# Order of issue and buffers of a linear-attention and Mish block taken from tables in place of a planner and pools

## The chip, the core and the metric

The kernel runs on one core of a Trainium2 chip. The metric is the device time of one execution in microseconds (us); lower is better. Before the change, three runs took 489.09, 489.33 and 489.36 us (median 489.33).

Engines are named as in the profile: PE is the matrix engine (PEld its weight loads), DVE the vector engine, ACT the scalar engine, POOL the general engine, SP the engine whose queue issues the DMAs. Each engine takes its instructions strictly in the order in which they were issued, and waits at the head of its queue until semaphores of the others let the next one go.

## What is computed

S is 2048 tokens, D 512, H 32 heads of 16, F 1792. In float32:

```python
xn = layernorm(x)
q, k, v = split(xn @ wqkv)                      # 32 heads of 16
phi(u) = [softmax(u @ w_phi), softmax(-u @ w_phi)]
kv = phi(k).T @ v ;  z = sum over tokens of phi(k)
o = (phi(q) @ kv) / (phi(q) @ z + 1e-6)
s = o @ wo
g = silu(mish(xn @ w1 + b1) @ w2)
out = x + s * g
```

## The kernel before

Tokens are worked on in 16 tiles of 128 (NT), and for the large products in pairs of tiles or in groups of 512. Each large product is taken in 2x2 blocks with seven block products in place of eight, and each float32 operand is split into a high and a low part of type fp32r (on ACT a copy to `...h`, on DVE or POOL the rest to `...l`), so that one block product is six matmuls: two halves of the contraction by three (low x high, high x low, high x high). Plain float32 matmuls are used for folding `w_phi` into the weights (`wkf`, `wqf`: a weight block times the block-diagonal `phit`), for transposes (`pt`), for `kvp` and for `pn`.

The program is written as parts, each a function of a tile or block number. In the order of the data:

- `N` normalizes a tile of x and transposes it (`pt`); the seven block operands of a pair of tiles are `fh`/`fl` (first and second group of 512 tokens) or `xc`.
- `kh`, `kl`, `wv`, `kd`, `ks`, `k2`, `k4` prepare the seven weight blocks for k and v, `wq` and `wQ` those for q. `wq` folds two chunks (`wqf`, through PSUM and an ACT copy) and stores them.
- `Ka` to `Kd` are the k and v products of a pair (banks `kx`, `ky`, `kz`; `kj` for the pair that is taken directly), with the softmax; `A` sums phi(k) and, for every second pair, multiplies into `kvp`. `z` ends the sums.
- `Q` is the q product of a pair of tiles (banks `qx`, `qy`, `qz`), its seven block products numbered Q.0, .2, .4, .6, .8, .10 and .12; `D` the denominator; `Ua`/`Ub` the numerator (`pn`, out into `oh` and `ol`); `O` the projection by wo (`pw`, stored as `so`).
- `P` prepares and `M` reloads the w1 blocks, `Fa` to `Fd` are the first product of the MLP (banks `fx`, `fy`, `fz`), stored raw as `hd`; `R` prepares w2.
- `G` is a step of the second product: `r` is loaded from `hd`, ACT applies Mish, three subtractions and sums make seven operands (`r` to `r`), then `ah` on ACT and `al` on DVE or POOL, and seven groups of matmuls into the `y` banks. `E` adds the banks up (`yc`, `yy`) and applies silu, `H` multiplies by `s`, adds x and stores. For the last 256 tokens one call, `G49`, does the seven sums in one pass at the end, and `E7` ends the four pieces one by one (`u`, `xx`).

What is recorded first is not yet an order. Every call on an engine goes to `Program.call`, which makes an operation of it; `one()` puts several calls into one operation, or gives one operation two possible engines (`either`: DVE or POOL; `copy`: ACT or DVE). Then `Program.order` decides. It hands PE its operations in the order of ORDER, the written list of parts; the other engines are filled by `simulate`, a list scheduler that plays the program with a cost for each operation (`cost`), due times (`late`, moved by the numbers in SHIFT), limits on free buffers (`fits`), a guard time for the port that DVE and POOL share, and a model of the DMA queue. What it returns, sorted by its start times, is issued. Where it has put an operation on POOL less than 4000 ns after the last DVE operation that takes two SBUF inputs (or the like) ends, `issue` adds a wait for that DVE operation.

Buffers come from pools: 8 PSUM banks under one tag, 38 large slots (`slot`), 15 of 2 KB (`s2`), and some small ones. The framework decides which buffer of its tag a tile gets.

Of the kernel before, what the change touches and what calls it, by code (L numbers as in the profile page):

```python
# [28 lines left out]
PEN, HOLD, MARGIN, GUARD = 0, 300, 1000, 140  # L29
BACK, COLD, DRATE, LANES, SWITCH = 2650, 3400, 400, 8, 230  # L30
READ, WRITE, STALL, AHEAD_PE = 1150, 150, 1500, 110
BLOCK, HEAD, FETCH, IDLE = 256, 89, 5200, 2100
BEGIN = {"PE": 1100, "V": 900, "G": 2300, "A": 800, "Q": 800}

SLOTS, S2 = 38,15
SLACK, AHEAD, LAT = 15000, 40000, 150
WAKE, EACH, NEAR = 15, 2, 4000
# [11 lines left out]
SHIFT = """  # L49
kd:0:-9100 wv1:0:-1100 N1:2:-15000 N1:3:300 N1:5:5800 N1:13:4300 N1:14:-7000 kl:3:-10000 Ka2:3:-9700 N5:6:-2200  # L50
N5:8:-1200 N5:11:13000 N2:0:-3500 N2:2:-2000 N3:4:1500 N3:13:-11400 Kc0:7:4900 Kc0:10:14200 k4:0:-6900 Kd0:6:300
N6:14:-6700 P0:1:4800 P0:5:3800 P0:11:5000 Kb1:3:300 N7:6:-2800 N7:8:7300 N7:9:-6400 N8:8:-2700 N9:13:3600 Kc1:8:1800
Kd1:4:-7300 N10:3:-300 N11:0:5800 P4:0:-7000 P4:4:300 P4:5:3100 N14:8:-6800 Kd3:1:-5000 Kd3:6:-6400 A2:0:-3600
N13:5:-2500 Fa4:1:-1100 Fa4:3:3600 N15:4:10800 N15:6:-5000 N15:11:-300 Kc5:6:4400 Ka6:1:-600 Kc6:5:-300 Kc6:6:2600
P6:6:-1100 P6:8:5100 P3:3:-2600 P3:11:-2000 Kb7:1:2800 Fa3:1:-300 Fa3:3:300 P2:4:-2000 P2:6:1100 P2:10:800 Kd6:6:-8800
Kd6:9:-9500 Fb6:3:-2300 Fc3:1:1600 Fc3:2:800 Fc3:4:7900 wQ:1:2300 wQ:13:6600 Fa2:3:300 Fa2:4:-1900 Fa1:3:900
M4:1:-1400 P5:10:3200 Q0:7:14700 Q0:23:-2000 z:4:1200 z:5:11100 D0:0:800 D0:4:4700 D0:8:-800 L:5:-4200 L:9:-3000
D1:2:-8100 Q1:16:800 Q1:19:300 Q2:3:-15000 Q2:9:-2500 Q2:15:300 Q2:25:-1900 Q3:17:-4300 Q3:18:4700 Fc5:5:9400
D3:7:1800 D4:3:-4000 D4:4:6800 D4:5:1300 D4:6:11900 D4:10:11500 D5:1:-300 Fb11:1:-4700 Q4:7:-600 Q4:16:600 Q4:18:7800
Q4:20:800 Q4:21:-1400 Q4:23:-8800 Q5:25:-600 M3:1:-5000 M3:2:-6700 Fa12:1:800 D6:6:-500 D6:10:300 Fb10:1:-500  # L60
D7:1:5000 D7:4:6600 D8:1:-2400 D8:4:-500 D8:10:1400 Q6:1:4700 D9:10:800 Q7:1:7800 Q7:16:-4700 Q7:20:4800 Q7:21:-13000
Q7:23:-12900 M2:2:-5000 D10:6:-800 M6:2:-4100 D11:1:-1700 Ua0:1:-1100 Ua0:12:-800 Fc9:1:3400 D12:5:-5000 D13:0:-4400
D13:4:12500 Fa13:4:800 Ub0:14:-4300 wo0:1:-4500 Fc13:4:-13100 Fc7:2:15000 R0:8:4700 D14:6:-7800 O3:2:-900 Ua1:2:-4200
Ua1:4:-6700 Ua1:6:-3100 Ua1:11:-5000 Ua1:13:-300 Ua1:14:300 O5:2:-500 Fd13:2:-4200 O6:1:-2200 Ub1:5:-5000 Ub1:6:-2000
Ub1:8:-4500 G7:4:-2000 R2:0:-2200 R1:1:15000 R1:6:4200 R1:10:5800 G8:3:-5000 G8:6:1900 O11:2:-2000 R6:1:4900 R3:2:1600
R3:8:-3300 R4:1:2000 G11:0:-6800 G12:5:3100 G12:6:-1200 G13:5:-1100 G32:3:6500 G34:6:4000 G1:4:-15000 G3:0:5000
G4:0:-4100 G5:5:4000 G35:3:9300 G35:4:-5800 G35:6:3100 G14:0:-10200 G14:3:4000 E0:6:-2600 G15:2:800 G39:6:-300
G16:4:-5000 G41:3:1700 E5:4:-300 G20:0:800 G20:2:-2000 G20:3:-5300 G20:6:-5000 G42:3:5100 G42:5:-300 G43:2:4200
G44:2:300 G44:4:-2000 H4:2:1300 G46:3:6600 G46:6:300 G24:6:500 G47:5:-3000 G26:4:-1600 E6:2:-800 G49:0:-5000
G49:2:4000 G49:6:-1100 G49:9:2000 G49:12:-2200 G49:19:2200 G49:26:5000 G49:31:800 G49:36:2800 G49:42:-4700 G49:43:800  # L70
E7:9:-300 E7:10:15000 H3:7:2300 H6:8:800
"""
ACT_SET = {AF.Exp: 1, AF.Silu: 3, AF.Mish: 2}


class Op:
    __slots__ = ("impl", "reads", "writes", "at", "idx", "succ", "ndep", "late", "new", "ready", "start", "eng", "sets", "slack", "open", "soon", "pos", "deps", "lock", "part", "half", "code", "tiles", "shift")


class Program:  # L80


    def __init__(self, nc):
        self.eng = {"PE": nc.tensor, "V": nc.vector, "G": nc.gpsimd, "A": nc.scalar, "Q": nc.sync}
        self.ops, self.tag, self.cap, self.pe = [], {}, {}, []
        self.group, self.slack, self.part, self.half = None, SLACK, None, False
        self.region, self.count = {}, {}
        self.shifts = {k: int(v) for k, _, v in (c.rpartition(":") for c in SHIFT.split())}

    @staticmethod  # L90
    def cost(e, m, a, k):
        aps = [v for v in a if isinstance(v, bass.AP)]
        n = aps[0].free_size()
        if e == "PE":
            if m == "transpose":
                return 109
            n, c = aps[2].free_size(), aps[1].free_size()
            if aps[1].dtype == F32R:
                return max(n / 2.4 + 0.104 * c, c * 0.835 + 2)
            full = 2 * max(n / 1.2 + 2.5, c * 0.835)  # L100
            if aps[1].shape[0] == 32:
                return max(0.155 * n, 24)
            return max(full * aps[0].shape[0] / P, 27)
        if e == "Q":
            return 450
# [29 lines left out]
    def add(self, impl, reads, writes, sets=()):  # L135
# [10 lines left out]
        if "PE" in impl:  # L146
            self.pe.append(o)
# [1092 lines left out]
```

## Time and profile before

| | before |
|---|---|
| median of 3 runs | 489.33 us |
| span of the profiled execution (first to last instruction) | 488.7 us |
| PE busy | 480.2 us (98%) |
| DVE busy | 446.2 us (91%) |
| ACT busy | 293.4 us (60%) |
| POOL busy | 267.2 us (55%) |
| DMA, mean over the span | 216 GB/s, 105.70 MB |

The page gives no time for the profiled execution other than its span.

In the rows below, the timeline has start (us), duration (us), engine, line, operation, what is written from what, shape, and in brackets the idle time before and what ended it. The chain of waits has start, duration, engine and tile. A row of a stretch has the stretch, its length, the busy time of PE, PEld, DVE, ACT and POOL in this order, the granted PE clock (1.00 is full), the share of time that the DMA engines were busy, and GB/s. A row of a group has the count, then the busy time and the mean of one in ns, or shortest, median and longest in ns. Nearly all work is recorded by one helper, so it carries that helper's line (L404), and one goes by the names of the tiles.

### The profile page before, as it was taken

To read this page: it belongs to the slowest core of one execution; us is meant where nothing else is said; L and a number is where in the kernel's file an instruction comes from. 1 tells how busy PE (TensorE), PEld (TensorE's weight loads), DVE (VectorE), ACT (ScalarE), POOL (GpSimd) and SP (SyncE) were. 2 spreads that over 40 slices of the span, in tenths; PEclk is the share of its full clock that TensorE was granted. 3 is DMA by queue.
4 is the path that set the end of the run, shared out by engine and by line. 5 is a ranking of instruction groups with operands and counts; after the bars stand their busy time and mean duration, and the time that the engine had idled before them with its cause. 6 is when DMAs were issued, how large, how long until landed. Compare 5 with 4: busy or idle time off the path is not lost.

```text
span 488.7 us, 10325 instructions
## 1 busy us (share of the span) xinstructions
PE 480.2 (98%) x3820; PEld 426.2 (87%) x3820; DVE 446.2 (91%) x893; ACT 293.4 (60%) x453; POOL 267.2 (55%) x197
## 2 busy tenths in 40 slices
PE   8899999999999999999999999999999999999996
PEld 7788888888887889898887878788899999999996
DVE  6999999988899999999999899889989889999894
ACT  3997545654556453635345545677879687777631
POOL 3989998998490446798987686370021024120030
PEclk9999999999999999999999999999999999999999
DMA  8812923968867689982959635726465646578172
GB/s 294 265 48 109 332 99 122 312 197 272 315 217 313 225 301 345 394 300 87 310 199 341 229 115 211 261 85 207 141 193 165 201 154 211 194 234 269 44 250 94
DMA packets 68641, 105.70 MB, mean 216 GB/s; under 512 B 6896, under 2 KB 37744, under 8 KB 68592
## 3 DMA queue, kind: packets, MB, share of 16 engines
q1 hardware_dynamic: 68448, 104.79, 62.9%
q8 instruction: 30, 0.49, 0.4%
q10 hardware_dynamic: 144, 0.26, 0.2%
q14 instruction: 19, 0.16, 0.1%
HBM read 60.60 MB, written 44.43 MB: 215 GB/s over the span
## 4 chain that ended last, share of the span: by engine, by line
PE 81%; DVE 8%; DMA 5%; issue 2%; ACT 1%; SPq 1%; POOL 1%; DVEq 0%; ACTq 0%
PE y L404 20%; PE fx L404 14%; PE pw L404 9%; PE kx L404 7%; PE fy L404 7%; PE qx L404 5%; PE ky L404 3%; PE fz L404 3%; PE qy L404 2%; PE kj L404 2%; PE pn L404 2%; PE kz L404 2%; DVE al L404 2%; DMA wvr<-wv 1%; DMA w1a<-w 1%
## 5 line engine op out<-in xcount | busy, mean ns | idle before, releaser
L404 POOL TENSOR_TENSOR al<-r,ah 128x896 fp32r<-128x896 f32 x8 | 17.0, 2130 | 87.4 <-DMA r<-hd 35.1
L404 ACT ACTIVATE ah<-r 128x896 fp32r<-128x896 f32 x56 | 50.9, 944 | 16.0 <-DVE r L404 12.9
L404 DVE TENSOR_TENSOR al<-r,ah 128x896 fp32r<-128x896 f32 x48 | 54.8, 1171 | 5.0 <-ACT ah L404 3.2
L404 DVE TENSOR_TENSOR r<-r 128x128 f32<-128x128 f32 (+1 forms) x157 | 48.3, 353 | 5.0 <-ACT r L404 3.4
L404 PE MATMUL y<-w2h,al 128*128 128x256 f32 x160 | 45.4, 283 | 0.0
L404 PE MATMUL y<-w2h,ah 128*128 128x256 f32 x160 | 45.3, 283 | 0.0
L404 PE MATMUL y<-w2l,ah 128*128 128x256 f32 x160 | 45.3, 283 | 0.0
L404 PE MATMUL y<-w2t,ah 128*128 128x256 f32 x224 | 41.0, 283 | 0.0
L404 PE MATMUL fx<-fh,w1b 128*128 128x512 f32 x112 | 38.8, 393 | 0.0
L404 ACT ACTIVATE r<-r 128x512 f32<-128x512 f32 x56 | 33.2, 621 | 7.9 <-DMA r<-hd 7.9
L404 PEld LDWEIGHTS y<-w2t,ah 128*128 128x128 f32 x224 | 34.9, 192 | 0.0
L404 PE MATMUL y<-w2t,al 128*128 128x256 f32 x112 | 31.7, 283 | 0.0
L404 PEld LDWEIGHTS y<-w2h,al 128*128 128x128 f32 x160 | 30.7, 192 | 0.6 <-issue 0.4
L404 PEld LDWEIGHTS y<-w2l,ah 128*128 128x128 f32 x160 | 30.7, 192 | 0.2
L404 PEld LDWEIGHTS y<-w2h,ah 128*128 128x128 f32 x160 | 30.7, 192 | 0.0
L404 PE MATMUL y<-w2g,ah 128*128 128x256 f32 x160 | 30.4, 283 | 0.0
L404 PEld LDWEIGHTS fx<-fh,w1b 128*128 128x128 f32 x112 | 21.0, 188 | 5.4 <-issue 1.2
L404 PEld LDWEIGHTS y<-w2g,ah 128*128 128x128 f32 x160 | 25.0, 192 | 0.0
L404 POOL TENSOR_TENSOR r<-r 128x128 f32<-128x128 f32 (+1 forms) x11 | 6.4, 592 | 32.3 <-DMA sr<-so 22.5
L404 PE MATMUL y<-w2g,al 128*128 128x256 f32 x80 | 22.6, 283 | 0.0
L404 ACT ACT_TABLE_LOAD x13 | 16.7, 1283 | 9.2 <-DMA x<-x 4.1
L404 PE MATMUL fx<-fl,w1b 128*128 128x512 f32 x56 | 21.8, 390 | 0.0
(766 smaller groups left out, 1730.0 us busy)
## 6 DMA issues: line engine op xcount, KB each, us to landing
r<-hd SPq DMA_DIRECT2D x56, 256.0 KB, 3.5
xd<-xc SPq DMA_DIRECT2D x8, 896.0 KB, 4.1
w1b<-w1d SPq DMA_DIRECT2D x14, 512.0 KB, 5.5
w1b<-w1d SPq DMA_DIRECT2D x14, 384.0 KB, 4.9
so<-so SPq DMA_DIRECT2D x16, 256.0 KB, 2.1
x<-x SPq DMA_DIRECT2D x15, 256.0 KB, 3.7
w1a<-w SPq DMA_DIRECT2D x7, 512.0 KB, 4.6
w1d<-w1sh SPq DMA_DIRECT2D x7, 512.0 KB, 2.9
```

Of the source, the lines that this page charges most:

```text
L404: ins = getattr(e, m)(*a, **k)
```

## The change

The scheduler goes. A table PLAN names every one of the 2454 operations in the order in which it is issued, over all engines, with a letter for the engine where there is a choice; a table PLACE names the buffer of every tile, tag by tag, in the order in which the tiles are made. Pools have one buffer per tag, and there is a tag for each buffer. The operations, their shapes and their number are the same; ORDER still sets in which order they are recorded (and so the buffer numbers in names), no longer that of PE.

```diff
-SLACK, AHEAD, LAT = 15000, 40000, 150
-WAKE, EACH, NEAR = 15, 2, 4000
+WAKE, EACH, NEAR = 15, 2, 24
...
-SHIFT = """
-kd:0:-9100 wv1:0:-1100 N1:2:-15000 N1:3:300 N1:5:5800 N1:13:4300 N1:14:-7000 kl:3:-10000 Ka2:3:-9700 N5:6:-2200
...
+PLAN = """
+N1.0 @.0 @.1 N4.0 @.2 @.3 @.15 @.4 N4.3 @.5 @.17 @.6 N0.0 @.7 N1.1 @.8 wv0.0 @.9 @.10 N1.2 @.11 @.16G N4.1 N1.3 @.12
...
+PLACE = {
+    "ps": """
+7 1 6 3 4 2 5 1 7 0 6 1 3 7 3 7 7 3 5 1 7 2 1 5 0 2 4 0 7 3 7 1 4 2 5 0 6 7 5 3 0 3 7 4 5 3 2 4 7 3 5 4 2 5 3 6 7 2 0
...
     def order(self):
-        at = [0]
-        for o in self.pe:
-            at.append(at[-1] + o.impl["PE"][0])
-        self.links()
-        return self.simulate(at)
...
+        at = {o.name: o for o in self.ops}
+        plan = []
+        for c in PLAN.split():
+            e = c[-1] if c[-1] in self.eng else ""
+            o = at.pop(c[:-1] if e else c)
+            o.eng = e or next(iter(o.impl))
+            plan.append(o)
...
     def issue(self, tc):
         first, held = True, None
-        for o in self.order():
-            for i, (m, a, k) in enumerate(o.impl[o.eng][1]):
+        for n, o in enumerate(self.order()):
+            for i, (m, a, k) in enumerate(o.impl[o.eng]):
...
-                if i == 0 and o.eng == "G" and held is not None and o.start - held[1] < NEAR:
+                if i == 0 and o.eng == "G" and m != "dma_start" and held is not None and n - held[1] < NEAR:
...
-    psum = ctx.enter_context(tc.tile_pool(name="psum", bufs=8, space=bass.MemoryType.PSUM))
+    psum = ctx.enter_context(tc.tile_pool(name="psum", bufs=1, space=bass.MemoryType.PSUM))
+    place = {t: iter(c.split()) for t, c in PLACE.items()}
...
-        pools[tag] = ctx.enter_context(tc.tile_pool(name=tag, bufs=n))
-        prog.cap[tag] = n
+        pools[tag] = ctx.enter_context(tc.tile_pool(name=tag, bufs=n if tag == "st" else 1))
...
-        t = psum.tile(shape, F32, tag="ps", name=name)
+        t = psum.tile(shape, F32, tag="ps" + next(place["ps"]), name=name)
...
-        t = pools[tag].tile(shape, dtype, tag=tag, name=name)
+        t = pools[tag].tile(shape, dtype, tag=tag if tag == "st" else tag + next(place[tag]), name=name)
```

The removed functions `cost`, `records`, `halves`, `links`, `simulate`, `volume`, `reads` and `bcast` served the scheduler alone. The wait of POOL for DVE is now added where at most 23 places of the list lie between the two.

131 operations change engine: 67 go from DVE to POOL, 42 from POOL to DVE, 13 from ACT to DVE, 9 from DVE to ACT. In the second product of the MLP, 47 sums and subtractions of `r` stand on POOL where 11 stood (36 of them 128x128, 11 of 128x256, against 6 and 5), and 1 split `al` where 8 stood. On PE about half of the operations keep their order among themselves; the others move, mostly by a few places, and by about 30 at most.

**Three places in the order.** The first is the start. The next two pieces are the first loads in SP's queue, before and now (x0 to x5 are tiles of x, wkT00 to wkT11 the four loads of wk, wvr0 and wvr1 the two halves of wv).

```order
L404 DMA x4_151<-x 128x512
L404 DMA x5_153<-x 128x512
L404 DMA phic_100<-phi 128x64
L404 DMA x0_164<-x 128x512
L404 DMA wkT00_137<-wqkT 128x512
L404 DMA wkT01_138<-wqkT 128x512
L404 DMA wvr0_141<-wv 128x2x512
L404 DMA wkT10_139<-wqkT 128x512
L404 DMA wvr1_159<-wv 128x2x512
L404 DMA wkT11_140<-wqkT 128x512
L404 DMA x2_202<-x 128x512
L404 DMA wqT10_190<-wqkT 128x2x512
```

```order
L294 DMA x4_151<-x 128x512
L294 DMA phic_100<-phi 128x64
L294 DMA x5_153<-x 128x512
L294 DMA wkT00_137<-wqkT 128x512
L294 DMA x0_164<-x 128x512
L294 DMA wvr0_141<-wv 128x2x512
L294 DMA wkT01_138<-wqkT 128x512
L294 DMA wkT10_139<-wqkT 128x512
L294 DMA wvr1_159<-wv 128x2x512
L294 DMA wkT11_140<-wqkT 128x512
L294 DMA wqT10_190<-wqkT 128x2x512
```

The first half of wv has moved ahead of wkT01, phic and wkT00 each by one place, and wqT10 ahead of x2.

On PE, in the same stretch, these are the first rows, before and now (wake keeps PE busy while nothing else is there).

```order
L404 MATMUL wake_99<-ones_84 128x128 x15
L404 MATMUL wkf01_147<-phit_101,wkT00_137 128x128 x4
L404 MATMUL wkf11_148<-phit_101,wkT01_138 128x128 x4
L404 MATMUL pt4_156<-ident_83,x4_151 128x128 x4
L404 MATMUL pt0_167<-ident_83,x0_164 128x128 x4
L404 MATMUL pt1_173<-ident_83,x1_170 128x128 x4
L404 MATMUL wkf21_181<-phit_101,wkT10_139 128x128 x4
L404 MATMUL wkf31_182<-phit_101,wkT11_140 128x128 x4
L404 MATMUL pt5_184<-ident_83,x5_153 128x128 x4
L404 MATMUL kx2_187<-wv0h_142,fl00_104 128x512
```

```order
L294 MATMUL wake_99<-ones_84 128x128 x13
L294 MATMUL wkf01_147<-phit_101,wkT00_137 128x128 x4
L294 MATMUL wake_99<-ones_84 128x128 x2
L294 MATMUL pt1_173<-ident_83,x1_170 128x128 x4
L294 MATMUL pt4_156<-ident_83,x4_151 128x128 x4
L294 MATMUL wkf11_148<-phit_101,wkT01_138 128x128 x4
L294 MATMUL pt0_167<-ident_83,x0_164 128x128 x4
L294 MATMUL wkf21_181<-phit_101,wkT10_139 128x128 x4
L294 MATMUL pt5_184<-ident_83,x5_153 128x128 x4
L294 MATMUL wkf31_182<-phit_101,wkT11_140 128x128 x4
L294 MATMUL kx2_187<-wv0h_142,fl00_104 128x512
```

The transpose pt5 has moved ahead of the last fold of wk (wkf31). A few rows on, still on PE, the two folds of wq stood one behind the other between kz2 and kj00; the piece before and the piece now:

```order
L404 MATMUL kz2_188<-wv1h_160,fl10_106 128x512
L404 MATMUL kz2_188<-wv1l_161,fh10_105 128x512
L404 MATMUL kz2_188<-wv1h_160,fh10_105 128x512
L404 MATMUL wqf21_192<-phit_101,wqT10_190 128x128 x4
L404 MATMUL wqf31_193<-phit_101,wqT10_190 128x128 x4
L404 MATMUL kj00_194<-wv0h_142,fl00_104 128x512
```

```order
L294 MATMUL kx2_187<-wv0h_142,fh00_103 128x512
L294 MATMUL wqf21_192<-phit_101,wqT10_190 128x128 x4
L294 MATMUL kz2_188<-wv1h_160,fl10_106 128x512
L294 MATMUL kz2_188<-wv1l_161,fh10_105 128x512
L294 MATMUL kz2_188<-wv1h_160,fh10_105 128x512
```

The fold wqf21 has moved ahead of kz2, and wqf31 is gone from here: it stands 18 matmuls after kz2, in the middle of kj03.

The second place is the q product on PE. Here is the end of the block of the first pair before (its last two block products, qy0 and qx0, one behind the other):

```order
L404 MATMUL qy0_525<-wqs1h_493,fl20_108 128x256
L404 MATMUL qy0_525<-wqs1l_494,fh20_107 128x256
L404 MATMUL qy0_525<-wqs1h_493,fh20_107 128x256
L404 MATMUL qx0_523<-wq1h_489,fl60_116 128x256
L404 MATMUL qx0_523<-wq1l_490,fh60_115 128x256
```

and what follows the same qy0 now:

```order
L294 MATMUL qy0_525<-wqs1h_493,fh20_107 128x256
L294 MATMUL fx2_512<-fh50_113,w1sl2_502 128x512
L294 MATMUL fx2_512<-fl50_114,w1sh2_501 128x512
L294 MATMUL fx2_512<-fh50_113,w1sh2_501 128x512
L294 MATMUL fx2_512<-fh50_113,w1sl2_502 128x512
L294 MATMUL fx2_512<-fl50_114,w1sh2_501 128x512
L294 MATMUL fx2_512<-fh50_113,w1sh2_501 128x512
L294 MATMUL qy2_606<-wqs0h_491,fl30_110 128x256
```

A block product of the MLP and one of another pair stand between, then qz0 and another of the MLP, before the last product of qx0 comes. The eight q blocks are mixed with the MLP in this way throughout.

The third place is on DVE, where the last numerator block (pn11) is split into the operands of the projection (ol), before and now.

```order
L404 TENSOR_TENSOR ol31_903<-pn11_1_897,oh31_902 128x8x32
L404 TENSOR_TENSOR ol21_901<-pn11_3_899,oh21_900 128x8x32
L404 TENSOR_TENSOR ol31_903<-pn11_2_898,oh31_902 128x8x32
L404 TENSOR_TENSOR w2m4_893<-w2e4_895,w2m4_893 128x256
L404 TENSOR_TENSOR ol31_903<-pn11_3_899,oh31_902 128x8x32
L404 TENSOR_TENSOR al1_2_937<-r1_2_935,ah1_2_936 128x896
```

```order
L294 TENSOR_TENSOR ol31_903<-pn11_1_897,oh31_902 128x8x32
L294 TENSOR_TENSOR ol21_901<-pn11_3_899,oh21_900 128x8x32
L294 TENSOR_TENSOR ol30_886<-pn10_3_882,oh30_885 128x8x32
L294 TENSOR_TENSOR r1_3_940<-r1_3_940 128x2x128
L294 TENSOR_TENSOR w2r6_927<-w2r6_927 128x256
L294 TENSOR_TENSOR ol31_903<-pn11_2_898,oh31_902 128x8x32
L294 TENSOR_TENSOR r4_1_970<-r4_1_970 128x2x128
L294 TENSOR_TENSOR w2e3_916<-w2r3_915,w2e3_916 128x256
L294 TENSOR_TENSOR r1_2_935<-r1_2_935 128x128
L294 TENSOR_TENSOR w2e6_928<-w2r6_927,w2e6_928 128x256
L294 TENSOR_TENSOR ol31_903<-pn11_3_899,oh31_902 128x8x32
```

The last piece of ol31 stood two places behind the one of pn11_2; now four other rows stand between, and it is the 605th row of DVE where it was the 587th. On PE the projections of tiles 8, 9, 12 and 15, which read ol21 and ol31, stand directly behind the first two steps of the second product, where only that of tile 8 and then 14 and 13 stood.

In the last stretch, E7's two copies of the first y bank go from ACT to DVE, and on DVE the sum for the third of the four last pieces (`u15_1`) is the ninth row from the end, where it was the fifth.

More of the change, by code (lines that the diff above doesn't have):

```diff
@@ L1 @@
 from contextlib import ExitStack, contextmanager
-import heapq
 import numpy as np
@@ L55 @@
[L55 to L64, printed above, removed]
@@ L76 @@
+E7.30
+"""
+PLACE = {
+    "ps": """
[4 rows of a table added]
+""",
+    "s2": """
[4 rows of a table added]
+""",
+    "slot": """
[11 rows of a table added]
+""",
+    "sm": """
[3 rows of a table added]
+""",
+    "tq": """
+1 0 1 0 0 1 0 1 0 1
+""",
+    "rq": """
+7 6 2 5 3 4 1 0 7 6 5 4 2 3 0 1
+""",
+}
 class Op:
-    __slots__ = ("impl", "reads", "writes", "at", "idx", "succ", "ndep", "late", "new", "ready", "start", "eng", "sets", "slack", "open", "soon", "pos", "deps", "lock", "part", "half", "code", "tiles", "shift")
+    __slots__ = ("impl", "reads", "writes", "idx", "name", "eng", "lock")
@@ L408, in issue @@
             if o.eng == "V" and "V" in o.lock:
-                held = ins.ins.name, o.start + o.impl["V"][0]
+                held = ins.ins.name, n
 def locks(e, m, a):
```

432 lines of the change are left out of this document (144 added, 288 removed), and 21 rows, old and new, of the table PLACE.

## The prediction

> **What bounds the kernel now.** I read the page's first rows, then the chain of waits over the stretch that looks densest, then the waits of each engine, then the two ends of the span in order of time.
>
> ```profile
> span 488.7 us, 10325 instructions
> PE 480.2 (98%) x3820; PEld 426.2 (87%) x3820; DVE 446.2 (91%) x893; ACT 293.4 (60%) x453; POOL 267.2 (55%) x197
> PEclk9999999999999999999999999999999999999999
> ...
> 297.70 13.60 PE pw L404 x60
> ...
> 355.62 85.45 PE y L404 x712
> ```
>
> TensorE is busy for 98% of the span at a granted clock of nine tenths or more in every slice. A busy PE may still stall, so I take its pace from long pieces of the chain: 60 matmuls of 512 columns in 13.60 us are 227 ns each, 712 of 256 columns in 85.45 us are 120 ns each. In 85 us nothing interrupts it. The same number of matmuls stands in the changed kernel, so this work is a floor that no order can lower. What an order can move is the time in which PE waits. That is found at the start, at a few places in the middle, and after the last matmul.
>
> ```profile
> 3.64 6.47 DMA wvr<-wv
> ...
> 10.13 1.07 ACT wv0h L404
> ...
> 11.27 0.76 POOL wv0l L404
> ...
> 13.60 2.41 POOL wv1l L404
> ...
> 16.06 1.42 PE kz L404 x5
> 17.48 0.91 PE wqf L404 x8
> ...
> 18.41 0.61 ACT wqf L404
> ...
> 19.06 1.16 PE wqf L404 x8
> 20.22 2.75 PE kj L404 x12
> ```
>
> This is the chain over the first 23 us: PE starts its long run (kj) only after a load of wv, its split on ACT and POOL, and two weight folds (wqf) with a copy on ACT between them.
>
> The page gives no execution time of its own beside the span. The median run took 489.33 us, 0.6 us over the 488.7 us span; I keep these 0.6 us and subtract from 489.3.
>
> **The change part by part. 1, the start.** The pieces of SP's and PE's order in the section on the change are priced with these:
>
> ```profile
> 12.67 1.16 PE L404 MATMUL wkf<-phit,wkT 128*128 128x128 f32 x8 [0.73 <-DMA wkT<-wqkT]
> 13.66 0.60 PE L404 MATMUL pt<-ident,x 128*128 128x128 f32 x4
> 14.02 0.48 PE L404 MATMUL kx<-wv0h,fl 128*128 128x512 f32 x1
> ...
> 12.00:14.00 2.00, 1.33 (x12) 1.33 (x13) 1.98 (x5) 2.00 (x5) 2.00 (x2) 1.00 1.05 408
> ...
> 19.97 0.48 PE L404 MATMUL kj<-wv0h,fl 128*128 128x512 f32 x1
> ```
>
> At 408 GB/s a load of 256 KB takes 0.64 us. The first wv load passes one such load (wkT01) in SP's queue, so it lands 0.64 us earlier, and wv0h, wv0l and wv1l follow: wv1l ends at 13.60+2.41-0.64=15.4. The last fold of wk waits for wkT11, ahead of which the same bytes stand, so it still starts at 12.67. What was behind it, pt5, is now ahead of it, and kx starts at 12.67+0.97=13.6 in place of 14.02. Six matmuls of 227 ns bring PE to 15.0, the first wqf fold (0.91) to 15.9, kz (1.36, wv1l long there) to 17.3. Then kj starts, against 19.97 before: 2.6 us earlier. Owed are the second fold (0.91), which comes later without ACT's 0.61 copy in front of it, and two more changes between plain and split matmuls (kj's first row lasts 0.48, its next ones 0.39, so 0.1 each). **Net -1.5 us.** Bounds: 0, if another producer (ACT's queue is in a new order too) is late by as much, and -2.0.
>
> **2, the middle.** Two kinds of stall are seen:
>
> ```profile
> 149.50 0.39 PE L404 MATMUL fz<-fh,w1ah 128*128 128x512 f32 x1
> 150.15 0.50 PE L404 MATMUL fx<-fh,w1al 128*128 128x512 f32 x1 [0.27 <-DVE w1al L404]
> ...
> PE fx L404 <- DVE w1al L404: 0.3, 1, 0.3
> ...
> 167.53 0.28 PE L404 MATMUL qy<-wqs1h,fh 128*128 128x256 f32 x1
> 167.68 0.39 PE L404 MATMUL qx<-wq1h,fl 128*128 128x256 f32 x1
> 167.90 0.28 PE L404 MATMUL qx<-wq1l,fh 128*128 128x256 f32 x1
> ```
>
> The start at 150.15 is 0.42 us late against the pace of 227 ns, and that row itself lasts 0.1 longer; in the list of PE's waits it is the longest one for DVE after the start. The prep1 of feature blocks 1 and 2 is spread differently now; I count **-0.5 us** (bounds 0 and -0.5). In each of the eight q blocks the last product reuses a bank just after DVE or ACT has read it: 0.15 and 0.22 us where the pace is 0.12, so 0.13 us, eight times 1.0 us. In the new order other products stand between these steps; I count **-1.0 us** (bounds 0 and -1.2).
>
> **3, the hand-over to the last product.**
>
> ```profile
> 140.00:170.00 30.00, 29.73 (x388) 25.04 (x387) 29.86 (x46) 15.67 (x24) 11.16 (x7) 1.00 0.73 270
> ...
> 326.12 0.41 DVE L404 TENSOR_TENSOR ol<-pn,oh 128x256 fp32r<-128x256 f32 x1
> 326.46 3.23 DVE L404 TENSOR_TENSOR al<-r,ah 128x896 fp32r<-128x896 f32 x1
> ```
>
> The last ol piece at 326.12 is the operand of the output projections. The order puts it 18 DVE rows later (587 to 605 from DVE's first), while products that need it (O12, O15) come forward on PE. Eighteen rows of 0.41 us would be 7 us if DVE did not run ahead; if it runs ahead with PE, nothing. New waits of PE here: 0 to +3.0 (all that PE has gained by then). I take **+0.8**, nearer to nothing, because DVE, busy 91% of the span, has idle time too, and part of that was waiting for PE.
>
> **4, work between DVE and POOL.** 131 of the operations that may run on two engines change theirs. The bulk lies in the last product, where the subtractions of r go to POOL (11 before, 47 now) and the splits al come back to DVE (8 on POOL before, 1 now).
>
> ```profile
> L404 POOL TENSOR_TENSOR r<-r 128x256 f32<-128x256 f32 x5 | 3.7, 742 | 9.8 <-DVE r L404 7.4 <-DVE w2m L404 2.4
> L404 POOL TENSOR_TENSOR r<-r 128x128 f32<-128x128 f32 x6 | 2.7, 467 | 22.5 <-DMA sr<-so 22.5
> ...
> L404 POOL TENSOR_TENSOR al<-r,ah 128x896 fp32r<-128x896 f32 x8 | 17.0, 2130 | 87.4 <-DMA r<-hd 35.1 <-DVE al L404 27.8 <-ACT ah L404 23.9
> ...
> L404 DVE TENSOR_TENSOR r<-r x152: 279/290/2210, 331.2 to 458.3; 128x128 f32<-128x128 f32 x101, 128x256 f32<-128x256 f32 x51
> L404 DVE TENSOR_TENSOR al<-r,ah x46: 1079/1085/3228, 326.5 to 463.1; 128x896 fp32r<-128x896 f32 x46
> ```
>
> DVE gains 7 al at 1.08 (+7.6 us) and loses 30 narrow r at 0.28 and 6 wide at 0.41, like the ol row of that size (-10.9): 3.3 us less. POOL's work goes by +30x0.467 +6x0.742 -7x2.13 = +3.6 us to 27. PE waits for neither in this stage, so I count **0**. What hides it is DVE's lead: the row of 330 to 450 us (its third busy time is DVE's, its fifth POOL's) shows 8.1 us idle in 120.
>
> ```profile
> 330.00:450.00 120.00, 120.00 (x931) 116.85 (x930) 111.92 (x239) 93.95 (x125) 18.43 (x14) 1.00 0.60 194
> ```
>
> The longest r on DVE took 2210 ns where 279 is the shortest, as long as a POOL al: so DVE can be held for a whole POOL operation. The Trainium skill ("SBUF — State Buffer", "SBUF: two separate sides") says that GpSimd and a DVE operation with two SBUF inputs share a port pair as an exclusive lock, and that the loser blocks for the whole instruction. By that rule the new POOL rows could hold DVE more often, though for 0.5 us each in place of 2.1; the 2210 ns agree with it. It speaks against this part, and its mechanism is the slower rival below.
>
> **5, buffers.** A table fixes which tile follows which in a buffer. In the list of PE's waits none before is for a buffer, the nearest is the 0.3 us above; the bounds are 0 and, at the hand-over, what term 3 holds already. I take 0. POOL's wait for DVE (now by places in the list) delays POOL alone.
>
> **6, the end.**
>
> ```profile
> 484.27 0.36 ACT L404 ACTIVATE u<-y 128x256 f32<-128x256 f32 x1
> ...
> 484.39 0.43 DVE L404 TENSOR_TENSOR u<-u,sr 128x256 f32<-128x256 f32 x1 [0.48 <-ACT u L404]
> ...
> 485.19 0.42 DVE L404 TENSOR_TENSOR u<-u,sr 128x256 f32<-128x256 f32 x1
> ```
>
> ACT ends its last silu at 484.63, but DVE takes the product at 485.19, since two rows of the preceding half stand before it. In the new order the sum for that half stands four rows earlier, so these rows are through sooner: **-0.4** (bounds -0.5 and +1.0, if DVE arrives at the end late, now that it also copies the two y tiles ACT copied).
>
> Sum: -1.5 -0.5 -1.0 +0.8 +0 -0.4 = -2.6, so 489.3-2.6 = **486.7 us**.
>
> **The rivals.** *DVE does not follow.* DVE is 91% busy over the whole span and 29.86 of 30 us in 140 to 170, where PE did wait for it. If its chain sets the hand-over, the 3.0 us gained earlier are spent there and only the end remains: 489.3-0.4 = 488.9 (488.0 to 489.6). Against it: the wait at 150 is 0.3 us, and no other for DVE is listed after the start. *Nothing happens:* the loads, not the order, set the start, and PE is full anyhow: 489.3. *Slower: POOL holds DVE through the last product.* Before, the longest r and al lie 4.1 us above the shortest ((2210-279)+(3228-1079) ns), beside 23.4 us of such work on POOL (17.0+2.7+3.7). If 85% of the new 27 us held DVE, that would be 23.0, 18.9 more; 3.3 less work and 8.1 idle leave 7.5. Of these 2.3 are covered at the last pass: the last al ends at 463.1+1.08=464.2, and the pass, 147 matmuls of 120 ns that end at 484.1, begins at 466.5. PE waits 5.2: 486.7+5.2 = 491.9. It decides from two thirds of POOL's time on. The Trainium skill's page named above states the hold as a rule. For it: the 2210. Against: most r took 290.
>
> **How the numbers follow.** The forecast has 0.60 (485.5 to 487.8), DVE does not follow 0.22, nothing happens 0.05, slower 0.13. A change of 0.2% is 1.0 us here, about what a measurement can tell from none. Faster takes the forecast and a quarter of the second case: 0.66; same the rest of it and the third: 0.20; slower 0.14. The bounds of the terms reach down to 489.3-4.2 = 485.1 and, with the hand-over full and the end late, up to 490.3; the range of 485.2 to 490.0 leaves out the slower case and a few in a hundred at either end.
>
> **What would show it.** Right: kj begins about 2.5 us earlier, no wait on PE at 150, q blocks without 0.22 us steps, the pace of 120 ns kept from 350 on. Wrong: PE waits for ol or al around 320 to 340; DVE rows of r or al far over 0.3 and 1.1 us in great number; a last al that ends less than 2 us before the last pass; ACT's queue late for kx.

## The result, and the profile after

| kernel | runs | median us | lowest to highest | ratio to before, 95% interval |
|---|---|---|---|---|
| before, beside it | 6 | 489.25 | 488.62 to 489.67 | 1 |
| changed | 6 | 493.33 | 490.06 to 494.16 | 1.0072 (1.0049 to 1.0094) |
| changed, timed again (after_again) | 8 | 491.77 | 490.21 to 493.63 | 1.0047 (1.0031 to 1.0064) |

The changed kernel is 0.5 to 0.7% slower, and its executions lie 4 us apart where those of before lie 1 us apart. The profiled one is the shortest of its six (490.06 us, span 488.3), so its profile shows the least of the loss. The page's first rows of the changed kernel, its first kj row and the list of PE's waits (us in total, times, longest):

```profile
span 488.3 us, 10248 instructions
PE 480.0 (98%) x3820; PEld 425.6 (87%) x3820; DVE 443.6 (91%) x872; ACT 286.2 (59%) x449; POOL 259.8 (53%) x222
...
16.80 0.39 PE L294 MATMUL kj<-wv0h,fl 128*128 128x512 f32 x1
...
PE pn L294 <- DVE ph L294: 1.5, 1, 1.5
...
PE y L294 <- DVE yy L294: 0.5, 1, 0.5
...
PE fx L294 <- DMA w1b<-w1d: 0.3, 1, 0.3
```

The long run of kj begins 3.2 us earlier than in the profile of before (19.97; 2.3 us earlier than in old_table, the same order in an execution of usual length, 19.10), but one wait for ph has come before the last two numerator blocks (309 us), and one for yy in the last product, where there was none.

To see where time goes I use PE's **lag**: the time passed, less the work done at its undisturbed pace (227 ns a matmul of 512 columns, 120 of 256, 110 of the plain 128 ones, 15 and 7 of those of pn and kvp, nothing for wake), summed over all PE rows up to a time. All profiles have the same 462.4 us of such work. Besides the two known profiles the table has the old order in an execution of usual length (old_table, below) and two more executions of the changed kernel.

| lag of PE at, us | 75 | 160 | 265 | 345 | last matmul | last matmul to end |
|---|---|---|---|---|---|---|
| before (span 488.7) | 11.7 | 16.4 | 17.8 | 21.7 | 21.7 | 4.5 |
| old_table (487.1) | 10.8 | 15.1 | 16.5 | 20.4 | 20.4 | 4.3 |
| changed (488.3) | 9.7 | 14.1 | 14.5 | 20.8 | 22.0 | 3.9 |
| after_again (488.5) | 9.9 | 14.2 | 14.6 | 20.5 | 22.1 | 4.0 |
| after_third (489.8) | 10.0 | 14.6 | 14.9 | 21.4 | 22.5 | 4.9 |

Against the old order in an execution of usual length, the changed kernel is 2.0 us ahead at 265 us. It loses 2.3 between 265 and 345, the hand-over, and 1.2 more in the last product, where the old order loses nothing.

In the last product DVE is no longer full, yet PE waits. The stretch of 330 to 450 us, and the r and al groups (shortest, median, longest in ns) of the changed kernel:

```profile
330.00:450.00 120.00, 119.45 (x925) 115.97 (x924) 102.95 (x197) 92.28 (x125) 27.57 (x43) 1.00 0.55 172
...
L294 DVE TENSOR_TENSOR r<-r x121: 274/288/595, 303.1 to 460.9; 128x128 f32<-128x128 f32 x76, 128x256 f32<-128x256 f32 x45
...
L294 DVE TENSOR_TENSOR al<-r,ah x55: 1075/1086/1353, 314.1 to 465.1; 128x896 fp32r<-128x896 f32 x55
```

DVE is busy for 103.0 us of the 120 where it was 111.9. POOL holds it less than before: the longest r is 595 ns in place of 2210, the longest al 1353 in place of 3228. So these operations are not late because POOL holds DVE. Here is the first change from one group of 512 tokens to another. The rows are DVE's (the copy of the finished bank y, the sums yc and yy that read the three others) and PE's from the same stretch:

```profile
362.77 1.09 DVE L294 TENSOR_TENSOR al<-r,ah 128x896 fp32r<-128x896 f32 x1 [0.81 <-ACT ah L294]
363.78 0.42 DVE L294 TENSOR_TENSOR r<-r 128x256 f32<-128x256 f32 x1
364.12 0.42 DVE L294 COPY yy<-y 128x256 f32<-128x256 f32 x1
364.57 0.42 DVE L294 TENSOR_TENSOR yc<-yy,y 128x256 f32<-128x256 f32 x1
365.09 0.69 DVE L294 TENSOR_TENSOR yy<-yc,y 128x512 f32<-128x512 f32 x1
365.82 1.02 DVE L294 TENSOR_TENSOR yy<-yy,y 128x256 f32<-128x256 f32 x2
...
363.92 0.39 PE L294 MATMUL y<-w2m,al 128*128 128x256 f32 x1
...
365.10 0.33 PE L294 MATMUL y<-w2h,al 128*128 128x256 f32 x1
...
366.38 0.36 PE L294 MATMUL y<-w2h,al 128*128 128x256 f32 x1
```

The al that ends at 362.77+1.09 = 363.86 is taken by PE at 363.92. The bank that yc has read by 364.57+0.42 = 364.99 is written at 365.10. The two orders run hand in hand, with nothing between. This place costs 0.2 us in this execution. The one listed wait for yy stands three changes of tokens later, at 428 us; here are DVE's rows ahead of it and PE's row:

```profile
422.08 0.41 DVE L294 TENSOR_TENSOR yy<-yy,y 128x256 f32<-128x256 f32 x1
...
423.63 2.09 DVE L294 TENSOR_TENSOR al<-r,ah 128x896 fp32r<-128x896 f32 x2
426.25 1.09 DVE L294 TENSOR_TENSOR r<-r 128x256 f32<-128x256 f32 x3 [0.54 <-ACT r L294]
427.26 1.01 DVE L294 TENSOR_TENSOR yy<-yy,y 128x512 f32<-128x512 f32 x2
...
427.99 0.39 PE L294 MATMUL y<-w2h,al 128*128 128x256 f32 x1 [0.55 <-DVE yy L294]
```

The group of tokens before it had its last matmul at 418 us, but its last two sums stand on DVE behind two al and five r (three of them shown), and PE's new group waits for the first of them. This wait is 0.7 of the 1.2 us that the last product loses; after_third has it too (0.6 listed). In after_again the one listed wait there is for an al, at the first change of tokens (364.61 us, 0.9).

For al, worked out in this way for all 49 steps (end of al to the first matmul that reads it), the old order has it ready a median of 12.5 us ahead (3.0 to 19.0), the changed one 1.9 (0.1 to 15.1).

### The profile page after: what moved, and what is told of

The parts are those of the page before. It is cut to its first block, busy times and chain, and to the rows that moved or that the text cites. A ratio compares the mean times of both kernels' runs of the same rounds, so it can differ in the third digit from the quotient of the medians.

```text
span 488.3 us, 10248 instructions
## 1 busy us (share of the span) xinstructions
PE 480.0 (98%) x3820; PEld 425.6 (87%) x3820; DVE 443.6 (91%) x872; ACT 286.2 (59%) x449; POOL 259.8 (53%) x222
## 4 chain that ended last, share of the span: by engine, by line
PE 85%; DMA 7%; DVE 5%; POOL 1%; ACT 1%; issue 0%; SPq 0%; DVEq 0%; POOLq 0%; ACTq 0%
PE y L294 27%; PE fx L294 14%; PE kx L294 7%; PE fy L294 7%; PE pw L294 5%; PE qx L294 5%; DMA r<-hd 4%; PE fz L294 4%; PE ky L294 3%; PE qy L294 2%; PE kj L294 2%; PE kz L294 2%; PE kvp L294 2%; PE pt L294 1%; PE qz L294 1%; PE pn L294 1%
## 5 line engine op out<-in xcount | busy, mean ns | idle before, releaser
L294 POOL TENSOR_TENSOR r<-r 128x128 f32<-128x128 f32 (+1 forms) x47 | 27.9, 612 | 106.9 <-DVE r L294 50.9
L294 DVE TENSOR_TENSOR al<-r,ah 128x896 fp32r<-128x896 f32 x55 | 59.5, 1094 | 11.3 <-ACT ah L294 9.5
L294 PE MATMUL y<-w2t,ah 128*128 128x256 f32 x224 | 42.5, 283 | 0.0
L294 DVE TENSOR_TENSOR r<-r 128x128 f32<-128x128 f32 (+1 forms) x121 | 36.5, 343 | 4.3 <-POOL r L294 3.2
L294 PE MATMUL y<-w2g,ah 128*128 128x256 f32 x160 | 31.4, 283 | 0.0
L294 PEld LDWEIGHTS y<-w2t,al 128*128 128x128 f32 x112 | 21.5, 192 | 0.0
```

The source lines that it names most:

```text
L294: ins = getattr(e, m)(*a, **k)
```

## The experiments

Unless a table of buffers is mentioned, these kernels take their buffers from pools of the old sizes. "Behind the first steps" means the 809 operations of the steps G0 to G6, G12 to G28 and G30 to G49 and of all E and H (the table has 2455 operations in all). Each table row has the median, its runs, and the ratio to the kernel before with its interval.

### Which half of the order, and the buffers

The first three kernels here change the order by halves, or the buffers alone.

```diff
 after_pools: buffers
-        t = pools[tag].tile(shape, dtype, tag=tag if tag == "st" else tag + next(place[tag]), name=name)
+        t = pools[tag].tile(shape, dtype, tag=tag, name=name)
 headA_tailB: PLAN behind the first steps, here DVE's rows from G12.6 on
-G12.6 G31.2 G13.4 G30.3 G4.2 G0.3 G0.4 G30.4 G13.6 G0.6
+G12.6 G11.6 G13.6 O12.1 O10.1 G30.2 G30.3 G30.4 G29.6 G30.6
 headB_tailA: the old order up to there, the new one behind
```

> The changed kernel once more, for a second profiled execution: the one at hand ran in 490.06 us, the others in 491.6 to 494.2. Theory 1 (no lead): in the last product its order has al ready a median of about 2 us before PE takes it, where it was 12, so every load or POOL operation that ends late reaches PE; an execution of 493 then shows 2 to 4 us more waits of PE after 340 us than the 1.3 us of the profile at hand, and no more before 300. Theory 2 (hand-over): the waits grow where the numerator meets the projections, 300 to 320 us (2.3 us at hand). Median 493.3 (490 to 494) by both.

> The order of the change, with buffers handed out by the framework from pools of the old sizes. Theory 3 (the fixed buffers come free late and hold back loads): 1 to 4 us faster than the changed kernel, and SP no longer waits 18 us at 267 us. Theories 1 and 2: as the changed kernel, 490 to 494.

> The order of the change up to the first steps of the last product, then the old order and engines for the 809 operations of the other steps (G0 to G6, G8 left out of none but G7 to G11 and G29, and all of E and H); pools. Theory 1: the lead of the old order is back, waits of PE after 340 us vanish, and the executions agree within 1 us: 486.5 to 488. Theory 2: 489 to 493, as wide as the changed kernel.

> The reverse: the old order up to the first steps of the last product, the order and engines of the change for the 809 operations behind; pools. Theory 1: start and middle of before, and the changed kernel's waits after 340 us: 490 to 494, executions apart by some us. Theory 2: 489.0 to 489.8, as steady as before.

| | us | runs | ratio |
|---|---|---|---|
| after_pools | 490.78 | 11 | 1.0027 (1.0014 to 1.0041) |
| headA_tailB | 488.19 | 10 | 0.9973 (0.9964 to 0.9983) |
| headB_tailA | 492.31 | 5 | 1.0059 (1.0047 to 1.0071) |

The loss is made behind the first steps: the old order there turns the changed kernel into one that is faster than before, and the new order there makes the old kernel 3.0 us slower. PE's list of headB_tailA for the last product (345 to 483 us) has mostly waits for al:

```profile
PE y L304 <- DVE al L304: 2.0, 2, 1.2
PE y L304 <- DVE yy L304: 0.2, 1, 0.2
```

The buffers are a smaller matter. The pools were 1.0 us below the table in this comparison, with intervals that overlap; the lag at 265 us is 13.6 with pools and 14.5 with the table.

### PE's order or that of the engines that feed it; POOL's share

```diff
 old_table: old order and engines in PLAN
 r_back_to_dve: 49 letters, order and table of buffers kept
-G28.2G ... G12.3G ... G13.3G ... G30.2G
+G28.2V ... G12.3V ... G13.3V ... G30.2V
 tail_feeders_old: as headA_tailB, but PE keeps the new order
 tail_pe_old: PE alone back to the old order behind the first steps, here from G13.13 on
-G13.13 G30.9 G0.12 G29.13 G30.12 G0.7 G0.13 G0.9 G0.8 G0.10 G1.9 G1.12
+G13.13 G29.11 G29.13 G30.7 G30.8 G30.9 G30.10 G30.11 G30.12 G30.13 G0.7 G0.8
```

> The old order and the old choice of engines on every engine, written into the table; pools. What is left of the change is only that no planner runs and that POOL's wait for DVE goes by 24 places. Theory 1 (no lead in the new order of the last product): no difference, 489.0 to 489.6. Theory 4 (the table's way of adding waits costs something): over 490. Its profile also shows the old order in an execution of the usual length; the one at hand had a span of 488.7 us where the executions just timed have 487.3.

> The changed kernel, its order and its buffers; only the subtractions and sums r of the last product are given back the engine that they had (42 from POOL to DVE, 7 the other way). Theory 5 (POOL's slow r rows, and DVE held by them, make al late): 2 us or more faster than the changed kernel (below 490), lead of al over 4 us. Theory 1: the rows stand at the same places and al as late as before in the row, so within 1 us of the changed kernel (491 to 493), lead about 2 us.

> The order of the change everywhere and PE's new order in the last product, but for the other engines (DVE, ACT, POOL, SP) the old order and engines in the same 809 operations of the last product; pools. Theory 1, if it is the order of the feeding engines that has lost the lead: 486.5 to 489, al ready 8 us or more ahead. Theory 6 (PE's new order asks for the steps' operands earlier): 490 to 493, lead about 2 us.

> The reverse: in those operations PE has its old order, DVE, ACT, POOL and SP the new one; pools. Theory 1 with the feeding engines: 490 to 493, lead about 2 us. Theory 6: 487 to 489.

| | us | runs | ratio |
|---|---|---|---|
| old_table | 489.36 | 11 | 1.0002 (0.9994 to 1.0011) |
| r_back_to_dve | 494.23 | 6 | 1.0094 (1.0072 to 1.0116) |
| tail_feeders_old | 491.99 | 6 | 1.0059 (1.0042 to 1.0076) |
| tail_pe_old | 488.23 | 12 | 0.9979 (0.9969 to 0.9988) |

That the order stands in a table costs nothing that these runs can tell. POOL's new r rows are not the loss: without them it is no smaller, in the medians it is larger. And my theory 1, the lost lead by the order of DVE, ACT and POOL, falls in the form that I had given it. With their old order al is ready a median of 9.2 us ahead, and the time is 492.0. With their new order and PE's old one the lead is 4.6 us and the time 488.2, with no wait of PE from 345 us on in the profile. In both comparisons with pools, then, PE's order alone decides: 490.8 (after_pools) and 492.0 with the new one, 488.2 (headA_tailB) and 488.2 with the old, whichever order feeds it.

### The mixing, the buffers of the new order, and a cut

In the new order the seven groups of matmuls of a step stand mixed with those of the next step.

```diff
 unmix, with the table of buffers: PE, here from G13.13 on
-G13.13 G30.9 G0.12 G29.13 G30.12 G0.7 G0.13 G0.9 G0.8 G0.10 G1.9 G1.12 G1.7 G1.13 G30.13 G0.11
+G13.13 G0.12 G0.7 G0.13 G29.13 G0.9 G0.8 G0.10 G0.11 G30.11 G30.9 G30.12 G30.13 G30.10 G30.7 G30.8
 pe_old_places: as tail_pe_old, with the table of buffers
 old_pe_mixed: old_table, PE alone in the new order behind the first steps
 cut265: new order for what the old kernel starts before 265 us, old order behind
```

> The changed kernel with its buffers, and every engine but PE in its order. On PE, in the last product behind its first steps, the seven groups of a step stand together again (steps in the order of the mean place of their groups); the new order mixes them with those of the next step. The first group of a step comes 4 groups of 3 matmuls later by this, about 1.5 us. Theory 6 (the mixing asks for al and for free y banks too early): 488.5 to 490, no waits of PE from 345 to 483 us, lead of al up from 2 to 3.5 us or more. Rival (the order of the steps or the hand-over costs): 491 to 493.

> As tail_pe_old (PE's old order in the last product, all else of the change), but with the table of buffers. Theory 3, small (the fixed buffers cost 0.4 to 1.0 us before 140 us, as the profiles show: 12.8 us lost by then with them, 11.9 without): 488.6 to 489.3. Without such a cost: 488.2.

> The old order on every engine, and only PE's order in the last product behind its first steps is the new, mixed one; pools. Theory 6: the old order's lead of 12 us covers al, so what is seen is the y banks: waits of PE for yc and yy of 1 to 3 us, 490 to 492. Rival (the mixing harms only together with the new order of the other engines): 489.0 to 489.6.

> The order of the change for the 1247 operations that the old kernel starts before 265 us, the old order and engines for the 1208 behind; pools. By the sums of the profiles the new order is 2.9 us ahead at 265 us with pools, and the old one loses 1.2 to 1.9 us less in the hand-over from 300 to 330: theory 7 (the rest of the loss is the hand-over, where SP stands 18 us before a load of w2 and DVE behind it makes ph late): 486 to 487, no wait for ph. Rival (the hand-over follows from PE being early, DVE gives the gain back there): 488 to 489.3.

| | us | runs | ratio |
|---|---|---|---|
| unmix | 496.31 | 6 | 1.0145 (1.0117 to 1.0173) |
| pe_old_places | 492.08 | 6 | 1.0055 (1.0037 to 1.0074) |
| old_pe_mixed | 493.26 | 6 | 1.0081 (1.0061 to 1.0101) |
| cut265 | 498.75 | 4 | 1.0193 (1.0173 to 1.0214) |

PE's waits from 345 us on in old_pe_mixed, and for 250 to 345 us in cut265:

```profile
PE y L304 <- DVE yc L304: 2.1, 2, 1.5
PE y L304 <- POOL al L304: 0.7, 1, 0.7
```

```profile
PE fz L304 <- ACT hd L304: 5.9, 1, 5.9
PE pn L304 <- ACT hd L304: 1.5, 1, 1.5
```

PE's new order alone costs the old kernel 4 us, and by the trace (3.7 us lost from 345 us on) most of that is waiting for y banks (yc), a smaller part for al; it is more than I had expected. Unmixing, which I expected to help, made it worse by 3 to 4.5 us, and the old PE order with the table came to 492.1 where with pools it is 488.2: both profiles show waits at y banks (yy and yc, 2.6 us listed in unmix, 2.0 in pe_old_places). In unmix more is lost behind the first two of these waits: between 366.3 and 369.7 us the granted clock is 0.50, and rows of 256 columns start 0.21 us apart where 0.12 is usual, some 1.5 us in all. unmix differs from unmix_pools below, and pe_old_places from tail_pe_old, by the table of buffers alone, and each is about 3.8 us slower than its partner. The table is made for one order of PE; that with another it holds back a bank that pools would have handed out fits these waits, but no run shows which bank. cut265 tells nothing of theory 7: its seam makes a wait of its own, 5.9 us for hd at 273 us, and from 276 us on the granted clock is 0.50 for 6.8 us.

### The gap before a bank is used again

The eight banks are full in the last product. The first matmul of a new group of tokens needs a bank that yc and yy of a finished group have read. I counted in PE's orders how many groups of three matmuls (0.36 us each) further on the first write of the next tokens stands than the last write into a bank of the finished ones (the banks of both taken in the order of these writes): 13 to 42 in the old order, 8 to 31 in the changed one, and in unmix 5 to 8 at its narrowest place, where G0 opens the new tokens ahead of G30, the last step of the tokens before. unmix_pools is unmix with pools; unmix_swap differs from it by these two steps alone:

```diff
 unmix_swap against unmix_pools: PE
-G13.13 G0.12 G0.7 G0.13 G29.13 G0.9 G0.8 G0.10 G0.11 G30.11 G30.9 G30.12 G30.13 G30.10 G30.7 G30.8
+G13.13 G29.13 G30.11 G30.9 G30.12 G30.13 G30.10 G30.7 G30.8 G0.12 G0.7 G0.13 G0.9 G0.8 G0.10 G0.11
```

> As unmix (on PE the seven groups of a step stand together), with pools in place of the table of buffers. Theory 6a (the mixing as such costs, by asking for al 1.5 us earlier): no waits of PE behind 345 us, 488 to 489. Theory 6b (what costs is the gap between the last matmul of a finished group of tokens and the first into the bank that it frees; the old order has 13 to 42 groups of 3 matmuls there, the changed kernel 8 to 31, this one 5 to 8 for the tokens of G0 and 12 or more for all others): one wait of 1 to 2 us for yy or yc near 364 us and none near 392, 408, 428 and 437 us; 489 to 490.5.

> As unmix_pools, but on PE the whole step G30 stands ahead of the whole step G0 (7 groups each change places, all other rows of all engines stay). The gap before the banks of G0's tokens goes from 5 to 8 groups to 13 to 15. Theory 6b: the waits for yy and yc near 364 us (2.3 us listed, 3.0 lost in all) go, and the time falls by about 3 us to 488.5 to 490. Rival (al of G30, now asked for 2.5 us earlier, or another part of the order): 491 to 493, with waits for al there.

| | us | runs | ratio |
|---|---|---|---|
| unmix_pools | 492.53 | 6 | 1.0064 (1.0043 to 1.0085) |
| unmix_swap | 489.24 | 11 | 1.0005 (0.9993 to 1.0017) |

PE's waits from 345 us on, first of unmix_pools, with its DVE and PE rows at the place, then of unmix_swap:

```profile
PE y L304 <- DVE yy L304: 2.0, 2, 1.3
PE y L304 <- DVE yc L304: 0.3, 1, 0.3
...
366.65 1.09 DVE L304 TENSOR_TENSOR al<-r,ah 128x896 fp32r<-128x896 f32 x1 [1.78 <-ACT ah L304]
367.66 0.41 DVE L304 TENSOR_TENSOR yy<-yy,y 128x256 f32<-128x256 f32 x1
...
368.12 0.38 PE L304 MATMUL y<-w2m,al 128*128 128x256 f32 x1 [1.32 <-DVE yy L304]
```

```profile
PE y L304 <- DVE al L304: 0.4, 1, 0.4
```

All bank waits of unmix_pools lie at the narrow place, and none at the four later changes of tokens, where it has 12 groups or more. They go with the swap, and so do 3.3 us of the median (3.1 when each is set against before beside it). Its median lies above what I had expected by either theory; the profile is of its shortest execution (490.43 us), and what the longer ones lose beside these waits is not shown. The rows show the mechanism too: the row that frees the last bank (yy at 367.66) stands on DVE behind an al that waited 1.78 us for ah. DVE takes its rows in order, so a late operand of one step holds back the bank of another, and PE asks for that bank at once.

The count alone doesn't tell where the changed kernel waits. In its first profile the narrow places (8 to 10 groups, at 365 and 392 us) cost 0.2 us or less each, and the wait at 428 us comes 27 groups after the last write into the bank. What counts is the gap set against the place of the reading sums in DVE's queue: there the two sums came 5 us behind the one before them. In the old order of PE that bank has 42 groups, and tail_pe_old, with DVE in the same new order, has no wait.

### The hand-over

Between 265 and 345 us the changed kernel loses 5.9 to 6.5 us in its three profiles, the old order 3.9. Of this difference, the wait for ph and the one for a load of w1b are in PE's list (1.5 and 0.3). SP stands for 18 us before a load of w2, which needs nothing but a free buffer, and further loads queue behind it (its rows, then the list of its waits). It is not the table of buffers that holds this load: with pools SP stands there for 16.8 us (after_pools), against what I had expected by theory 3. Next are ACT's rows and DVE's row behind that load:

```profile
266.56 0.88 SPq L294 DMA_DIRECT2D hd<-hc  x2
285.48 0.38 SPq L294 DMA_DIRECT2D w2r<-w  x1
...
SPq L294 <- PE fy L294: 18.2, 2, 18.0
```

```profile
298.08 1.06 ACT L294 ACTIVATE w2h<-w2r 128x1024 fp32r<-128x1024 f32 x1 [4.92 <-POOL w2r L294]
...
300.39 0.38 ACT L294 ACTIVATE oh<-pn 128x256 fp32r<-128x256 f32 x1
...
300.81 0.42 DVE L294 TENSOR_TENSOR ol<-pn,oh 128x256 fp32r<-128x256 f32 x1 [2.67 <-ACT oh L294]
```

ACT waits 4.92 us for the late w2 before it comes to oh, and DVE 2.67 for oh, with the denominators and ph of the last pairs behind it. The edit moves three operations:

```diff
 handover_fix (on tail_pe_old) and after_fix (on the changed kernel): ACT, then DVE
-R0.5 O3.1 Fd7.1 R0.9 Ub0.15
+Ub0.15 R0.5 O3.1 Fd7.1 R0.9
-G8.2 D13.7 D15.4 D14.7 D14.8 R1.3 D15.5 G8.3 D15.6 D13.8
+D13.7 D15.4 D14.7 D14.8 R1.3 D15.5 D15.6 D13.8 G8.2 G8.3
```

> As tail_pe_old, with three operations moved: on ACT the copy oh of the last numerator piece of tile block 1 goes ahead of w2h, which waits for a late load of w2; on DVE two r of G8, which wait for a load of hd, go behind q13e. Theory 7 (in-order queues behind those loads make ph late): the wait for ph (1.7 us in tail_pe_old) is gone or under 0.5, and with the old order of PE behind it nothing takes it back: 486.6 to 487.4. Rival (DVE is full there, ph is late anyhow): 488.0 to 488.5.

> The changed kernel with the same three operations moved, its buffers and all else kept. Theory 7: the wait for ph is gone as in handover_fix; theory 6b: but PE comes to the first change of tokens earlier, where the bank is not free earlier, so the gain is given back in part: 490.5 to 492.5 (the changed kernel 491.8 to 493.3). If all of it stayed: 490.5.

> The changed kernel, a third look. If the execution is one of the longer ones (492 or more), theory 6b expects its further waits of PE at the changes of tokens near 364, 393, 408, 428 and 438 us (for yy, yc or al), not before 300 us.

| | us | runs | ratio |
|---|---|---|---|
| handover_fix | 488.03 | 10 | 0.9975 (0.9964 to 0.9985) |
| after_fix | 492.88 | 6 | 1.0067 (1.0053 to 1.0081) |
| after_third | 491.47 | 1 | |

The listed wait for ph falls from 1.7 us (tail_pe_old) to 0.6, but a wait of 0.4 us comes up in the last numerator block that the list puts down to nothing it shows (issue). PE's lag at 345 us falls from 20.1 to 19.7; the median moves 0.2 us, less than the intervals. So theory 7 is right on the chain to ph and wrong on what it is worth, and most of the hand-over's loss stays. In handover_fix the idle time before ol is gone, but just behind it a row of DVE that takes 0.23 us in the changed kernel takes 1.86, and ends where a row of POOL ends (DVE's rows, then POOL's):

```profile
297.42 0.41 DVE L304 TENSOR_TENSOR ol<-pn,oh 128x256 fp32r<-128x256 f32 x1
...
298.37 1.86 DVE L304 TENSOR_TENSOR tz<-tz,q15r 128x64 f32<-128x64 f32 x1
...
297.76 2.39 POOL L304 TENSOR_TENSOR w2l<-w2r,w2h 128x1024 fp32r<-128x1024 f32 x1
```

On the changed kernel itself the edit brings nothing that the medians show (492.88 against 491.77 and 493.33). Of after_third, whose span is 1.5 us longer than that of the first profile, 0.5 us lie ahead of 160 us, 0.2 in the hand-over, and 1.0 behind the last matmul, while the middle and the last product lose 0.1 less each (rows of the lag table): no single place. Where executions of 493 and 494 us lose theirs isn't shown by any profile of the unedited kernel. A lower clock doesn't explain them: the one of 493.68 us had a mean granted clock of 1.000, as the shortest one had.

## Why the prediction was wrong

Slower by 0.5 to 0.7% came out where 0.5% faster was forecast, and the time lies above the range. By the prediction's own steps, against old_table:

- **The base.** I took the profiled execution of before as usual, 0.6 us below the median. The executions timed beside the change show 1.9 to 2.0 us between span and time (a span of 487.3 for 489.25), so that profile, with 488.7, was some 1.3 us longer than usual. (For the changed kernel the difference is 1.7 to 1.8.) Part of what I saw to gain, at the start above all (lag 11.7 at 75 us, 10.8 usually), wasn't there.
- **1, the start**, -1.5: -1.1 at 75 us (-2.0 against the longer profile). Right in kind, though kj came earlier than forecast (16.80 us for 17.3).
- **2, the middle**, -1.5: -0.9 from 75 to 265 us. The q blocks give their 1.0 (the lag grows by 0.4 from 160 to 265, where it grew by 1.4). The 0.5 of the stall at 150 was given back. From 75 to 160 us the lag grows by 3.8 to 3.9 in all eight profiles of the new order with pools, but by 4.3 to 5.2 in six of the seven with the table (3.8 in unmix), where the old order has 4.3. So the fixed buffers, which I put at 0, most likely cost this part.
- **3, the hand-over**, +0.8 (0 to +3.0): +2.3, inside the bounds, but this is partly luck, since it came by another chain. PE waited 1.5 us for ph ahead of the last two numerator blocks, not for the late ol of the last one (which by the rows of the profiles stands 15 operations later on DVE, 597th to 612th, not 18). What made ph late were in part w2 loads behind an 18 us stand of SP, and ACT's queue behind them; with that chain shortened (handover_fix) only 0.4 us came back, so the rest is open.
- **4, DVE and POOL in the last product**, 0: POOL was no loss (r_back_to_dve). The step that failed is the cover: "what hides it is DVE's lead". I took that lead from the old trace (12.5 us by the count above) as given; it came from the old order and did not outlive it (1.9 us).
- **5, buffers**, 0, failed together with that cover, and the two decided. "None before is for a buffer" was true, and it was so because the old PE order left 13 or more groups before a bank was used again. I showed the mixing of PE's order for the q blocks, where it helps, and did not read it in the last product, where PE comes to banks and to al sooner than DVE has them ready. That is +1.1 to +1.6 us in the three profiles. headB_tailA (waits mostly for al) and old_pe_mixed (mostly for banks) put it at 3 to 4 us in the median. The table of buffers, also in this term, adds 1.0 by the medians of after_again and after_pools, where the intervals overlap.
- **6, the end**, -0.4: -0.4 and -0.3 in two profiles of the changed kernel, +0.6 in the third.

The medians add up: +3.0 for the new order of the last product (headB_tailA), -1.1 for all that stands ahead of it (headA_tailB) and +1.0 for the table of buffers make +2.9, and +2.5 and +4.1 were measured. The forecast had -2.2 ahead of the last product, nothing in it, and -0.4 at the end.

Of the rivals, the slower one named a time near the measured (491.9), but by POOL holding DVE, and that isn't what happened: the longest r and al on DVE got shorter. "DVE does not follow" had right that the gain (2.0 us at 265) is spent again in the hand-over (2.3), and stopped short of the last product.

The version that keeps the new order's gains and gives back its loss is tail_pe_old or headA_tailB, both with pools, 0.2 to 0.3% faster than before, and 0.7 to 1.0% faster than the changed kernel by the medians.

## What to carry to other kernels

A list of waits with no entry for a buffer says only that the present order leaves room; before the order of the busy engine is changed, count in it how much work stands between the last use of each scarce buffer and the next, and compare with the time at which its readers come, by their place in their own engine's queue and not by their length alone. An order in which operands and banks come just in time can look nearly as good in its best execution (490.1 us, where the old kernel took 488.5 to 490.8) and be worse in the others (up to 494.2): slack that costs nothing in the profile is worth keeping. And a table of buffers belongs to one order: both times that PE's order was edited under it, the kernel was about 3.8 us slower than the same order with pools, where the order it was made for is 1.0 us slower.

## What the runs showed that I had not expected

- The old kernel's profile came from an execution 1.3 us longer than its usual ones; a comparison of two profiles alone would have called the change 0.4 us faster (488.3 against 488.7) while the medians say 2.5 to 4.1 slower.
- Two steps of seven groups, exchanged on PE, are worth about 3 us of 490 (unmix_pools and unmix_swap).
- A 128x64 operation on DVE took 1.86 us where 0.23 is usual (handover_fix, 298 us), as the longest r of before had (2210 ns for 279). The rule of the Trainium skill ("SBUF — State Buffer", "SBUF: two separate sides"), a hold for the whole of a GpSimd instruction, fits both lengths: the row of 1.86 us ends at 300.23 beside POOL's w2l, which runs from 297.76 to 300.15. No run took the two apart. In the changed kernel, with four times as many r rows on POOL, no r of DVE took over 595 ns.
